# Layer-norm means of the first two tiles in two halves on two engines, and the first load split over two queues

## Chip, cores, metric

The kernel runs on one core of one Trainium2 chip. The metric is device time in microseconds (us). The engines are PE (TensorE), DVE (VectorE), ACT (ScalarE), POOL (GpSimd) and SP (SyncE, which here only starts DMAs).

## The reference

```python
xn = _layernorm(x)                    # x: [1, 2048, 512] bf16, over the last axis
return x + A(xn) + B(xn)              # A: linear attention with softmax features, 32 heads
                                      # B: ((xn @ w_gate) * (xn @ w_up)) @ w_down
```

Everything starts from the layer norm. The kernel works on 16 tiles of 128 tokens by 512. Only the mean has to be subtracted before the first products; the division by the deviation is done later ("deferred").

## The kernel before

A small recording layer notes every operation with its reads and writes; a list scheduler orders each engine, except where `sc.pin` keeps the written order. All that matters here is pinned.

```python
    load_x(0, 2)                      # tiles 0 and 1 in one DMA, 256 KB, SyncE's queue
    load_v(SP, 0)                     # V weights, first half
    load_x(2, 2)                      # tiles 2 and 3
    load_gu(SP, 0, (1,))              # first slice of the up weights
    act(sbf("lnv", 0, 1), eps_f, ["eps"], ["pace"])
    load_v(ACT, 1)                    # V weights, second half, ScalarE's queue
    load_gu(ACT, 0, (0,))             # first slice of the gate weights, ScalarE's queue
    # ... cut ...
    def ln_moments(t):                # VectorE: bn_stats, bn_aggr
        dve(lambda e: e.bn_stats(stats_v[:, t, 0:6], x_tile(t)), [("x", t)], [("st", t)], 512)
        dve(lambda e: e.bn_aggr(mv_v[:, t, :], stats_v[:, t, 0:6]), [("st", t)], [("mv", t)], 1)
    def ln_mean(t):                   # ScalarE: a sum over 512 by the accumulator
        act(xn_tile(t), x_tile(t), [("x", t)], [("mu", t)], scale=1.0 / 512.0, accum=mu[:, t:t + 1])
    # ... cut ...
    warm(7)                           # matmuls on constants, they wait for nothing
    warm(2, 512, [("x", 0)])          # two more once x is there
    sc.pin = True
    ln_moments(0)
    ln_mean(1)
    ln_center(0, 2)                   # x - mean, in two halves
    ln_center(1, 2)
    x_transpose(0, 2, 0, 2)           # four calls: tiles 0 and 1 on PE, by halves
    # ... cut ...
    v_matmul(0, 0)                    # V products of tiles 0 and 1: eight matmuls of 512 columns
    v_matmul(1, 1)
    ln_moments(2)
    ln_mean(3)
    ln_center(2)
    ln_center(3)
    ln_moments(1)
    ln_moments(3)
    # ... PE then: first half of the gate product, transposes of tile 2, next gate half,
    #     transposes of tile 3, and from there a dense stream of matmuls to the end
```

The softmax here doesn't subtract the row's maximum and nothing guards it: scores larger than these inputs give would overflow.

## Time and profile before

| | before |
|---|---|
| time, 3 runs | 221.35 us (221.35 to 221.50) |
| time of the profiled execution | 221.54 us |
| x0 and x1 land / tiles 2 and 3 land | 4.28 / 7.34 us |
| first transpose / first V product / tile 2's transposes | 5.59 / 6.35 / 8.73 us |

Two lines of the page, the span and the chain of work that ended last, by engine:

```profile
span 219.8 us, 3293 instructions
...
PE 96%; DMA 2%; issue 1%; DVE 1%
```

PE sets the time. Next, the timeline of PE alone in the first microseconds: start, duration, engine and line, what it did, and in brackets how long the engine had been idle and what ended that.

```profile
0.82 3.15 PE L640 MATMUL ps<-const-bfloat16-1.0 128*128 128x512 bf16 x7 [0.82 <-PEq L883]
4.32 0.61 PE L640 MATMUL ps<-const-bfloat16-1.0 128*128 128x512 bf16 x2 [0.35 <-DMA arena<-in_A_x_dram]
5.59 0.87 PE L417 MATMUL ps<-arena 128*128 128x128 bf16 x8 [0.66 <-DVE arena L385]
6.35 2.34 PE L222 MATMUL ps<-arena 128*128 128x512 bf16 x12
8.73 0.40 PE L417 MATMUL ps<-arena 128*128 128x128 bf16 x4
8.96 0.60 PE L222 MATMUL ps<-arena 128*128 128x256 bf16 x4
```

L640 are the warm-up matmuls, L417 the transposes. The twelve of L222 are eight V products, 0.216 us apart, and the first gate half, four of 0.109. The single records put the last of these at 8.42, so PE stood still for 0.2 us before 8.73. (Matmul durations overlap: each V product is recorded as 0.38 us long. Distances between starts tell the rate.) What it waited for is on VectorE:

```profile
4.30 0.69 DVE L360 BATCH_NORM_STATS2 arena<-arena 128x6 f32<-128x512 bf16 x1 [4.30 <-DMA arena<-in_A_x_dram]
5.03 0.18 DVE L361 BATCH_NORM_AGGREGATE arena<-arena 128x2 f32<-128x6 f32 x1
5.25 0.87 DVE L385 TENSOR_SCALAR arena<-arena 128x256 bf16<-128x256 bf16 x4
6.30 0.49 DVE L426 COPY arena<-ps 128x256 bf16<-128x256 bf16 x2 [0.18 <-PE ps L417]
7.37 0.69 DVE L360 BATCH_NORM_STATS2 arena<-arena 128x6 f32<-128x512 bf16 x1 [0.58 <-DMA arena<-in_A_x_dram]
8.10 0.18 DVE L361 BATCH_NORM_AGGREGATE arena<-arena 128x2 f32<-128x6 f32 x1
8.32 0.62 DVE L385 TENSOR_SCALAR arena<-arena 128x512 bf16<-128x512 bf16 x2
```

Tile 2 lands at 7.34; its statistics start at 7.37, and aggregate and centering lead to its transposes 1.36 us after that. The transposes start about 0.41 us after VectorE starts centering tile 2 (8.32 and 8.73). So two things meet at 8.73: PE's own work from x0 on, and the load of tile 2.

### The profile page before, as it was taken

To read this page: it belongs to the slowest core of one execution; us is meant where nothing else is said; L and a number is where in the kernel's file an instruction comes from. 1 tells how busy PE (TensorE), PEld (TensorE's weight loads), DVE (VectorE), ACT (ScalarE), POOL (GpSimd) and SP (SyncE) were. 2 spreads that over 40 slices of the span, in tenths; PEclk is the share of its full clock that TensorE was granted. 3 is DMA by queue.
4 is the path that set the end of the run, shared out by engine and by line. 5 is a ranking of instruction groups with operands and counts; after the bars stand their busy time and mean duration, and the time that the engine had idled before them with its cause. 6 is when DMAs were issued, how large, how long until landed. Compare 5 with 4: busy or idle time off the path is not lost.

```text
span 219.8 us, 3293 instructions
## 1 busy us (share of the span) xinstructions
PE 214.4 (98%) x1251; PEld 105.0 (48%) x1275; DVE 141.3 (64%) x245; ACT 86.2 (39%) x162; POOL 53.6 (24%) x119
## 2 busy tenths in 40 slices
PE   6999999999999999999999999999999999999995
PEld 1664444444444444544444444544454444454453
DVE  2766999876546654675486565797766777445341
ACT  4568774787343435333445525531122211000000
POOL 3030553332022202220241422224332222200000
DMA  6999715298200000000002220343764545342221
GB/s 182 295 302 297 198 43 121 59 336 185 49 0 0 0 3 0 0 0 3 0 0 48 49 47 4 71 74 76 163 144 100 118 106 115 87 102 73 61 61 49
DMA packets 47104, 19.90 MB, mean 91 GB/s; under 512 B 37488, under 2 KB 46448, under 8 KB 47088
## 3 DMA queue, kind: packets, MB, share of 16 engines
q1 hardware_dynamic: 46288, 19.16, 36.0%
q10 hardware_dynamic: 800, 0.52, 0.8%
q8 instruction: 10, 0.16, 0.3%
q14 instruction: 6, 0.05, 0.1%
HBM read 8.67 MB, written 2.10 MB: 49 GB/s over the span
## 4 chain that ended last, share of the span: by engine, by line
PE 96%; DMA 2%; issue 1%; DVE 1%
PE ps L222 91%; PE ps L539 2%; PE ps L492 2%; DMA arena<-in_A_x_dram 2%; PE ps L333 1%; PE ps L417 1%; DVE arena L360 0%; DVE arena L385 0%; DVE arena L621 0%; DVE arena L361 0%
## 5 line engine op out<-in xcount | busy, mean ns | idle before, releaser
L222 PE MATMUL ps<-arena 128*128 128x512 bf16 (+3 forms) x938 | 204.8, 371 | 1.3
L222 PEld LDWEIGHTS ps<-arena 128*128 128x128 bf16 x962 | 90.8, 98 | 98.2 <-ACT arena L203 0.2
L203 ACT ACTIVATE arena<-ps 128x512 bf16<-128x512 f32 (+2 forms) x114 | 63.0, 593 | 87.3 <-PE ps L222 74.3
L597 DVE TENSOR_TENSOR arena<-ps,arena 128x512 bf16<-128x512 f32 x56 | 38.5, 687 | 21.8 <-PE ps L222 18.0
L447 DVE TENSOR_REDUCE arena<-arena 128x64 f32<-128x1024 bf16 x32 | 38.5, 1213 | 20.9 <-ACT arena L203 20.9
L457 POOL TENSOR_TENSOR arena<-arena 128x512 bf16<-128x512 bf16 x32 | 33.9, 1060 | 1.3
L455 POOL TENSOR_TENSOR arena<-arena 128x32 f32<-128x32 f32 x32 | 8.6, 268 | 91.2 <-DVE arena L451 50.8
L621 DVE TENSOR_TENSOR arena<-ps,arena 128x512 bf16<-128x512 f32 (+2 forms) x13 | 8.5, 650 | 21.5 <-PE ps L222 21.5
L203 ACT ACTIVATE arena<-arena 128x512 bf16<-128x512 bf16 (+3 forms) x29 | 14.4, 508 | 5.8 <-DMA arena<-in_A_x_dram 2.8
L360 DVE BATCH_NORM_STATS2 arena<-arena 128x6 f32<-128x512 bf16 x16 | 10.4, 674 | 5.0 <-DMA arena<-in_A_x_dram 4.9
L203 ACT ACTIVATE arena<-ps,arena 128x512 bf16<-128x512 f32 x16 | 10.1, 685 | 5.7 <-PE ps L222 5.7
L560 DVE TENSOR_TENSOR arena<-ps,arena 128x512 bf16<-128x512 f32 x16 | 11.1, 691 | 0.6
L480 DVE TENSOR_TENSOR arena<-ps,arena 128x512 bf16<-128x512 f32 x16 | 10.3, 643 | 0.0
L451 DVE RECIPROCAL arena<-arena 128x64 f32<-128x64 f32 x16 | 8.4, 533 | 0.0
L492 PEld LDWEIGHTS ps<-arena 128*128 128x128 bf16 x128 | 6.2, 97 | 3.8
L539 PEld LDWEIGHTS ps<-arena 128*128 128x128 bf16 x128 | 6.2, 97 | 3.8
L397 POOL TENSOR_SCALAR arena<-arena 128x1 f32<-128x1 f32 x12 | 3.0, 269 | 17.7 <-ACT arena L203 17.7
L539 PE MATMUL ps<-arena 128*128 128x68 bf16 x128 | 6.7, 194 | 0.0
L492 PE MATMUL ps<-arena 128*128 128x68 bf16 x128 | 6.7, 194 | 0.0
L559 DVE RECIPROCAL arena<-arena 128x32 f32<-128x32 f32 x16 | 5.6, 353 | 0.5
L453 DVE RECIPROCAL arena<-arena 128x32 f32<-128x32 f32 x16 | 5.4, 344 | 0.2
L474 POOL CAST arena<-arena 128x32 bf16<-128x32 f32 x16 | 5.2, 322 | 0.0
(30 smaller groups left out, 34.0 us busy)
## 6 DMA issues: line engine op xcount, KB each, us to landing
out_dram<-arena SPq DMA_DIRECT2D x15, 128.0 KB, 1.7
arena<-in_B_w_down_dram SPq DMA_DIRECT2D x1, 1792.0 KB, 8.0
arena<-in_A_x_dram SPq DMA_DIRECT2D x3, 512.0 KB, 3.7
arena<-arena SPq DMA_TRANSPOSE x44, 2.8
arena<-in_B_w_gate_dram SPq DMA_DIRECT2D x1, 640.0 KB, 8.9
arena<-in_B_w_up_dram SPq DMA_DIRECT2D x1, 640.0 KB, 10.0
arena<-in_A_x_dram SPq DMA_DIRECT2D x2, 256.0 KB, 4.6
arena<-in_B_w_gate_dram SPq DMA_DIRECT2D x1, 512.0 KB, 5.4
```

The lines of the kernel that those rows point to most:

```text
L203: return sc.step(ACT, lambda e: e.activation(out=out_ap, in_=in_ap, func=func, scale=scale, **kw), reads, writes, 130.0 + 0.833 * n)
L222: ins = e.matmul(out_ap, lhsT=l, rhs=r, start=start and i == 0, stop=stop and i == npair - 1, **kw)
L360: dve(lambda e: e.bn_stats(stats_v[:, t, 0:6], x_tile(t)), [("x", t)], [("st", t)], 512)
L447: dve(lambda e: e.tensor_reduce(out=sm, in_=e_v, axis=AX.X, op=ALU.add), [(name, s, 0), (name, s, 1)], [("sums", sr)], 1024)
L455: pool(lambda e: e.tensor_tensor(out=rat, in0=sm[:, :, 0], in1=rs[:, :, 1], op=ALU.mult), [("sums", sr), ("rs", s)], [("rat", s)], 32)
L457: pool(lambda e: e.tensor_tensor(out=e_v[:, :, 1, :], in0=e_v[:, :, 1, :], in1=rat[:, :, None].to_broadcast([128, H, 16]), op=ALU.mult), [ ...
L480: dve(lambda e: e.tensor_tensor(out=vs_tile(t)[:, :, 0:16], in0=bank(b).rearrange("p (h f) -> p h f", h=H), in1=rp.unsqueeze(2).to_broadca ...
L492: ins = e.matmul(bank(c // 4, (c % 4) * CW, CW), lhsT=ek[:, c * 128:(c + 1) * 128], rhs=vs[:, c * CW:(c + 1) * CW], start=(t == 0 and c % ...
L539: ins = e.matmul(bank(b0 + c // 4, (c % 4) * CW, CW), lhsT=ph[:, c, :], rhs=kvz_v[:, c, :], start=True, stop=True)
L560: dve(lambda e: e.tensor_tensor(out=o_tile(t).rearrange("p (b h f) -> p b h f", b=2, f=16), in0=nd[:, :, :, 0:16], in1=w_v[:, r].unsqueeze ...
L597: dve(lambda e: e.tensor_tensor(out=hT_v[:, ft, sg * 512:(sg + 1) * 512], in0=bank(bu), in1=g, op=ALU.mult), [("ps", bu), ("g", s)], [("hT ...
L621: dve(lambda e, ps=ps, stg=stg, cs=cs: e.tensor_tensor(out=stg, in0=ps, in1=x_tile(t)[:, cs], op=ALU.add), [("ps", bk), ("x", t)], [("ostg ...
```

## The change

The intent: center tile 0 sooner, by loading it alone and by summing its two halves on two engines at once, and push the statistics, needed only later, out of the way.

```diff
-    load_x(0, 2)
+    load_x(0, 1)
+    load_x(1, 1, ACT)
...
+    def ln_mean_split(t):
+        act(xn_tile(t)[:, 256:], x_tile(t)[:, 256:], [("x", t)], [("mu", t)], scale=1.0 / 512.0,
+            accum=mu[:, t:t + 1])
+        dve(lambda e: e.tensor_scalar(out=xn_tile(t)[:, :256], in0=x_tile(t)[:, :256], scalar1=1.0 / 512.0,
+                                      scalar2=0.0, op0=ALU.mult, op1=ALU.add, accum_out=mua[:, t:t + 1]),
+            [("x", t)], [("mua", t)], 256)
+    def ln_center_split(t):
+        for h in range(2):
+            hs = slice(h * 256, (h + 1) * 256)
+            dve(lambda e, hs=hs: e.tensor_scalar(out=xn_tile(t)[:, hs], in0=x_tile(t)[:, hs], scalar1=mua[:, t:t + 1],
+                                                 scalar2=mu[:, t:t + 1], op0=ALU.subtract, op1=ALU.subtract),
+                [("x", t), ("mua", t), ("mu", t)], [("xn", t, h)], 256, 0.27)
...
-    warm(2, 512, [("x", 0)])
+    warm(1, 512, [("x", 0)])
     sc.pin = True
-    ln_moments(0)
-    ln_mean(1)
-    ln_center(0, 2)
-    ln_center(1, 2)
+    ln_mean_split(0)
+    ln_center_split(0)
+    ln_mean_split(1)
+    ln_center_split(1)
...
     v_matmul(1, 1)
+    ln_moments(0)
     ln_moments(2)
```

The change also takes one warm-up matmul away, and it puts a load ahead of V's and the gate weights on ScalarE's queue.

More of the change, by code (lines that the diff above doesn't have):

```diff
@@ L162, in _build @@
     alloc("mu", 2 * ND)
+    alloc("mua", 2 * ND)
     alloc("nrstd", 2 * ND)
@@ L375, in ln_stats @@
         sc.prio = 1
+    mua = sbf("mua", 0, ND)
+    def ln_mean_split(t):
[10 more added lines that the diff above has]
+                [("x", t), ("mua", t), ("mu", t)], [("xn", t, h)], 256, 0.27)
     def ln_mean(t):
```

## The prediction

> **What bounds the kernel now.** The tensor engine: the page's busy shares give PE 98% of a 219.8 us span; the chain that ended last is 96% PE. From 5.59 us on, the timeline of the matmuls shows nearly no hole. So the change can win only before about 9 us; nothing later gets shorter.
>
> **The start before (timeline, chain).** The 256 KB load of tiles 0 and 1 is issued at 0.79 us and lands at 4.28. VectorE: statistics 4.30 (0.69 us), aggregate 5.03 (0.18), four centerings 5.25 to 6.12. PE: transposes 5.59, V products 6.35 (eight of 0.216), first gate half 8.09 to 8.53, then a hole of 0.2 us, and tile 2's transposes at 8.73. That hole is a second bound: tiles 2 and 3 land at 7.34, and statistics, aggregate and centering of tile 2 take 1.36 us from there.
>
> **The change, costed.**
> - x0 alone is 128 KB. The packet records show x0 and x1 in 2 KB packets of about 84 ns, first at 1.82, typically done by 2.9, slowest 3.9. Half of it should land at about 3.6 (3.3 to 4.0). x1, from ScalarE's queue, at about 4.0. [...] the two queues' loads are served in order of issue (ScalarE's first packet starts at 2.96, as x's load ends). The order changes: tiles 2 and 3 now come before the first gate weights, 256 KB earlier; at the 330 GB/s of these microseconds about 0.7 us, so at 6.6, while gate weights slip from 6.63 to 7.3.
> - Half a mean: ScalarE 0.33 + 0.18 = 0.51 us (512 elements took 0.72), VectorE about 0.45 at the same time, in place of 0.95 for statistics and aggregate. Tile 0's centering starts at about 4.2.
> - Tile 1 gains less: its VectorE half stands behind tile 0's centerings; it is centered by about 5.5.
> - Moved, not removed: tile 0's statistics and aggregate (0.95 us) now stand ahead of tile 2's on VectorE, from about 6.2 to 7.1. So tile 2's statistics start at about 7.1 instead of 7.37, though x is there at 6.6.
> - One warm-up matmul of 0.22 us goes from a hole: free.
>
> **On the critical path.** Transposes of tile 0 come about 1 us earlier, V products and gate half 0.6; then PE waits for tile 2, whose transposes come only 0.2 to 0.4 us earlier. The whole PE stream behind shifts by that. Most of what is won in front is lost in that wait.
>
> **Predicted:** 221.05 us (0.3 us less), range 220.4 to 221.6. Faster by over 2%: 1%; within 2%: 98.5%; slower: 0.5%.
>
> **What would show each step.** x0 landing near 3.6; first centering 4.2; first transpose 4.5; V products 5.7; x2 landing 6.6; tile 2's statistics 7.1, right behind the moved ones; a hole of 0.4 to 0.6 us before tile 2's transposes, at 8.3 to 8.5; everything after shifted alike.
>
> **What would make it wrong.** ScalarE's issue may wait behind its table load, or its packets interleave with x0's; the accumulating VectorE half may be slow (over 0.5 us); late V or gate weights may hold PE; the PE clock: [...] Here matmuls went from 0.427 us apart to 0.22 between 3.3 and 4.5 us; less warm-up could delay that. Other instruction orders later, from the list scheduler, could move some tenths either way.

Two passages, on the queues and on the PE clock, are cut where marked, because no trace of this case shows what they said. The sum comes to 221.05 us, 0.3 less than 221.35.

## The result

221.63 us (median of 6, 221.28 to 222.14) against 221.41 (6 runs, 221.35 to 221.50). The ratio is 1.0011, interval 0.9997 to 1.0024. A ratio is the mean time of one kernel's runs over that of the other's runs of the same rounds, so not quite the ratio of the medians quoted. That is the same time within noise, 0.2 us up instead of 0.3 down, and just above the stated range (221.6). What stands out is the spread: 0.86 us where the kernel before had 0.15.

The profiled execution happened to be the fastest, 221.28 us. Its page:

```profile
span 219.5 us, 3324 instructions
...
PE 95%; DVE 2%; DMA 1%; issue 0%; ACT 0%; DVEq 0%
```

PE alone:

```profile
0.82 3.57 PE L658 MATMUL ps<-const-bfloat16-1.0 128*128 128x512 bf16 x8 [0.82 <-PEq L902]
4.50 0.62 PE L435 MATMUL ps<-arena 128*128 128x128 bf16 x4
5.47 0.54 PE L435 MATMUL ps<-arena 128*128 128x128 bf16 x4 [0.36 <-DVE arena L391]
5.85 2.46 PE L223 MATMUL ps<-arena 128*128 128x512 bf16 x12
8.41 0.40 PE L435 MATMUL ps<-arena 128*128 128x128 bf16 x4
8.64 0.60 PE L223 MATMUL ps<-arena 128*128 128x256 bf16 x4
```

And VectorE (L384 is the half mean, L391 the centering with two scalars, L362 the statistics: first tile 0's, then tile 2's):

```profile
3.48 0.42 DVE L384 TENSOR_SCALAR_CACHE_REDUCE arena<-arena 128x256 bf16<-128x256 bf16 x1 [3.48 <-DMA arena<-in_A_x_dram]
3.82 0.08 DVE L384 DVE_READ_ACCUMULATOR arena<-arena 128x1 f32 x1
4.10 0.60 DVE L391 TENSOR_SCALAR arena<-arena 128x256 bf16<-128x256 bf16 x2 [0.19 <-ACT arena L204]
4.61 0.41 DVE L384 TENSOR_SCALAR_CACHE_REDUCE arena<-arena 128x256 bf16<-128x256 bf16 x1
4.95 0.08 DVE L384 DVE_READ_ACCUMULATOR arena<-arena 128x1 f32 x1
5.07 0.60 DVE L391 TENSOR_SCALAR arena<-arena 128x256 bf16<-128x256 bf16 x2
...
6.26 0.69 DVE L362 BATCH_NORM_STATS2 arena<-arena 128x6 f32<-128x512 bf16 x1
6.98 0.18 DVE L363 BATCH_NORM_AGGREGATE arena<-arena 128x2 f32<-128x6 f32 x1
7.08 0.66 DVE L362 BATCH_NORM_STATS2 arena<-arena 128x6 f32<-128x512 bf16 x1
7.77 0.18 DVE L363 BATCH_NORM_AGGREGATE arena<-arena 128x2 f32<-128x6 f32 x1
7.99 0.62 DVE L403 TENSOR_SCALAR arena<-arena 128x512 bf16<-128x512 bf16 x2
```

In this execution nearly every step came as forecast: first centering 4.10, V products 5.85, x2 landing 6.69, its statistics 7.08 right behind the moved ones, its transposes 8.41. Against the profiled execution of before that is 0.32 us at the transposes and 0.26 us in time (221.28 against 221.54). So the question is not whether that chain exists but what the other executions do.

**One rule for all runs.** Sixteen profiles were taken in the end. In each, the time is the start of tile 2's transposes plus 212.81 to 212.94 us. Behind that point all the kernels run alike; only what comes before it counts.

| kernel | warm-ups | gate weights by | x2 lands | gate weights land | tile 2's transposes | time of that run | difference |
|---|---|---|---|---|---|---|---|
| before | 9 | ScalarE | 7.34 | 6.63 | 8.73 | 221.54 | 212.81 |
| after | 8 | ScalarE | 6.69 | 7.66 | 8.41 | 221.28 | 212.87 |
| r1_after | 8 | ScalarE | 7.80 | 9.22 | 10.29 | 223.18 | 212.89 |
| r2_warm | 9 | ScalarE | 6.67 | 8.04 | 8.53 | 221.38 | 212.85 |
| r3_gate_behind | 8 | SyncE | 6.90 | 7.79 | 9.84 | 222.69 | 212.85 |
| r4_load_only | 9 | ScalarE | 6.83 | 7.83 | 8.32 | 221.26 | 212.94 |
| r5_before_warm1 | 8 | ScalarE | 7.45 | 6.70 | 8.82 | 221.64 | 212.82 |
| r6_stats_behind | 9 | ScalarE | 7.95 | 9.38 | 9.87 | 222.73 | 212.86 |
| r7_mean_only | 9 | ScalarE | 7.22 | 6.51 | 9.11 | 221.93 | 212.82 |
| r8_warm4 | 11 | ScalarE | 7.49 | 8.92 | 9.41 | 222.28 | 212.87 |
| r9_gate_fill | 9 + 1 | SyncE | 6.40 | 7.34 | 8.61 | 221.47 | 212.86 |
| r10_fill | 9 + 1 | ScalarE | 7.35 | 8.50 | 8.99 | 221.84 | 212.85 |
| r11_gate_fill_behind | 9 + 1 | SyncE | 6.42 | 7.27 | 7.98 | 220.83 | 212.85 |
| r12_split_one_queue | 9 + 1 | ScalarE | 7.42 | 5.98 | 9.06 | 221.94 | 212.88 |
| r13_gate_nine | 9 | SyncE | 6.43 | 7.34 | 8.67 | 221.55 | 212.88 |
| r14_load_gate | 9 | SyncE | 6.28 | 7.10 | 8.33 | 221.17 | 212.84 |

(Landings are the last of the 16 completions of a load in the trace's landing records; "+ 1" is a warm-up matmul between the transposes of tiles 0 and 1.)

### The profile page after: what moved, and what is told of

The parts are those of the page before. It is cut to its first block, busy times and chain, and to the rows that moved or that the text cites. A ratio compares the mean times of both kernels' runs of the same rounds, so it can differ in the third digit from the quotient of the medians.

```text
span 219.5 us, 3324 instructions
## 1 busy us (share of the span) xinstructions
PE 215.8 (98%) x1274; PEld 105.0 (48%) x1274; DVE 142.2 (65%) x249; ACT 86.4 (39%) x164; POOL 53.6 (24%) x119
## 3 DMA queue, kind: packets, MB, share of 16 engines
HBM read 8.67 MB, written 2.10 MB: 49 GB/s over the span
## 4 chain that ended last, share of the span: by engine, by line
PE 95%; DVE 2%; DMA 1%; issue 0%; ACT 0%; DVEq 0%
PE ps L223 90%; PE ps L557 2%; PE ps L510 2%; DMA arena<-in_A_x_dram 1%; PE ps L335 1%; DVE arena L362 1%; PE ps L435 0%; DVE arena L391 0%; DVE arena L444 0%; ACT arena L204 0%; DVE arena L384 0%; DVE arena L363 0%; DVE arena L403 0%; DVE arena L639 0%; DVEq L875 0%
## 5 line engine op out<-in xcount | busy, mean ns | idle before, releaser
L223 PE MATMUL ps<-arena 128*128 128x512 bf16 (+3 forms) x962 | 207.2, 371 | 0.0
L223 PEld LDWEIGHTS ps<-arena 128*128 128x128 bf16 x962 | 90.8, 98 | 98.3 <-DMA arena<-in_B_w_gate_dram 0.5
L204 ACT ACTIVATE arena<-arena 128x512 bf16<-128x512 bf16 (+4 forms) x30 | 14.6, 497 | 5.3 <-POOL arena L415 2.6
L362 DVE BATCH_NORM_STATS2 arena<-arena 128x6 f32<-128x512 bf16 x16 | 10.4, 671 | 0.3 <-DMA arena<-in_A_x_dram 0.3
L568 POOL TENSOR_SCALAR arena<-arena 128x32 f32<-128x32 f32 x4 | 1.2, 293 | 16.3 <-DVE arena L465 16.3
```

The lines of the kernel that those rows point to most:

```text
L204: return sc.step(ACT, lambda e: e.activation(out=out_ap, in_=in_ap, func=func, scale=scale, **kw), reads, writes, 130.0 + 0.833 * n)
L223: ins = e.matmul(out_ap, lhsT=l, rhs=r, start=start and i == 0, stop=stop and i == npair - 1, **kw)
```

## The experiments

Each kernel ran five timed rounds beside the kernel before on the same chip; all gave correct results.

| kernel | median (range), runs | before, same chip | ratio (95% interval) |
|---|---|---|---|
| r1_after | 222.12 (221.23 to 223.18), 6 | 221.35 | 1.0033 (1.0008 to 1.0058) |
| r2_warm | 221.57 (221.38 to 221.64), 5 | 221.35 | 1.0007 (0.9995 to 1.0019) |
| r3_gate_behind | 221.98 (221.17 to 223.07), 6 | 221.35 | 1.0030 (1.0002 to 1.0058) |
| r4_load_only | 221.61 (221.26 to 221.70), 5 | 221.35 | 1.0011 (0.9998 to 1.0024) |
| r5_before_warm1 | 221.61 (221.49 to 222.85), 6 | 221.45 | 1.0023 (1.0003 to 1.0043) |
| r6_stats_behind | 221.79 (221.09 to 222.73), 6 | 221.45 | 1.0017 (1.0000 to 1.0033) |
| r7_mean_only | 221.91 (221.58 to 223.00), 6 | 221.45 | 1.0025 (1.0009 to 1.0040) |
| r8_warm4 | 221.88 (221.48 to 222.65), 6 | 221.45 | 1.0018 (1.0004 to 1.0033) |
| r9_gate_fill | 221.34 (221.22 to 221.47), 5 | 221.50 | 0.9995 (0.9982 to 1.0007) |
| r10_fill | 221.90 (221.79 to 222.06), 5 | 221.50 | 1.0020 (1.0007 to 1.0032) |
| r11_gate_fill_behind | 221.09 (220.83 to 221.35), 5 | 221.50 | 0.9986 (0.9973 to 1.0000) |
| r12_split_one_queue | 221.94 (221.90 to 222.16), 5 | 221.50 | 1.0023 (1.0010 to 1.0035) |
| r13_gate_nine | 221.43 (221.32 to 221.55), 5 | 221.42 | 1.0001 (0.9988 to 1.0013) |
| r14_load_gate | 220.87 (220.56 to 221.17), 5 | 221.42 | 0.9974 (0.9961 to 0.9988) |

### First call: what makes the runs differ?

**r1_after**: the changed kernel, unaltered.

> The changed kernel again, for its spread (its six runs gave 221.28 to 222.14 us, those of the kernel before 221.35 to 221.50). Theory LOADS: the loads of tiles 2 and 3 (SyncE, issued at 1.71 us) and of the first gate weights (ScalarE, issued at 1.74 us) are in a tie, and which is served first differs from run to run; where the gate weights go first, x2 lands some 0.7 us later and with it all that follows. It expects the same spread again, 221.2 to 222.2, and, if the profile falls on a slow run, x2 landing at 7.2 or later in place of 6.69. Theory CLOCK: the work now starts before the matmul clock is up in some runs; then a slow run shows V products 0.427 us apart in place of 0.216, and x2 at 6.7. Theory NOISE: the spread was chance, and all runs lie at 221.2 to 221.5.

The spread is real and wider: 221.23, 221.31, 221.70, 222.54, 222.81, 223.18. The profile caught the slowest. PE in it:

```profile
0.82 3.57 PE L658 MATMUL ps<-const-bfloat16-1.0 128*128 128x512 bf16 x8 [0.82 <-PEq L902]
4.71 0.65 PE L435 MATMUL ps<-arena 128*128 128x128 bf16 x4 [0.31 <-DVE arena L391]
5.68 0.65 PE L435 MATMUL ps<-arena 128*128 128x128 bf16 x4 [0.32 <-DVE arena L391]
6.13 4.33 PE L223 MATMUL ps<-arena 128*128 128x512 bf16 x12
10.29 0.39 PE L435 MATMUL ps<-arena 128*128 128x128 bf16 x4
```

The same twelve matmuls of L223 take 4.33 us instead of 2.46. The single records show all eight V products 0.427 us apart, and the gate half 0.213: half rate until about 10.2 us. In the fast execution the rate had doubled between 4.84 and 5.47. NOISE falls. The eight V products lose eight times 0.211 us, 1.7 in all, but not all of it reaches tile 2, because in the same profile x2 (7.80) and the gate weights (9.22) are over a microsecond late too. In r6 and r8 below, where the V products run at full rate, tile 2's transposes start 0.49 us after the gate weights land. By that the landing alone would have put them at about 9.7 here (an estimate). So of the 1.9 us between 223.18 and 221.28 about 1.3 goes with the landing, and the half rate adds the last 0.6.

**r2_warm**

```diff
-    warm(1, 512, [("x", 0)])
+    warm(2, 512, [("x", 0)])
```

> The changed kernel with the ninth warm-up matmul given back. CLOCK expects the spread to vanish, all runs at 221.2 to 221.4 us. LOADS expects the same spread as r1_after, 221.2 to 222.2.

The spread went (0.26 us), as CLOCK says. The level, 221.57, is above its forecast of 221.2 to 221.4 and above before. In the profile, PE waits 0.24 us for the gate weights, which land at 8.04.

**r3_gate_behind**

```diff
-    load_gu(SP, 0, (1,))
+    load_gu(SP, 0)
...
-    load_gu(ACT, 0, (0,))
```

> The changed kernel with the load of the first gate weights taken from ScalarE's queue and put on SyncE's, behind the load of tiles 2 and 3, so that there is no tie. LOADS expects x2 to land at 6.3 to 6.8 us in every run, the spread to shrink to 0.3 us or less and the median to lie at 221.0 to 221.4. CLOCK and NOISE expect no change against r1_after.

LOADS, in this form, fell: x2 landed at 6.90 close to what it expected, but the runs are 221.17, 221.26, 221.28, 222.69, 222.92, 223.07. The profile (222.69) again has V products 0.427 us apart, up to 9.1 us. Here the landings are not to blame: VectorE starts centering tile 2 at 8.30, so its transposes could have come at about 8.7 (an estimate, by the 0.41 us above) instead of 9.84. The late clock cost about 1.1 us. But note the gap: nothing lies between 221.28 and 222.69. The in-between runs of the changed kernel (221.55 to 221.85) are missing here.

**r4_load_only**: the kernel before with `load_x(0, 1)` and `load_x(1, 1, ACT)` alone.

> The kernel before with the split load alone (x0 on SyncE, x1 on ScalarE; statistics, mean and warm-up as before). LOADS expects the spread here too: about 220.7 us where x2 lands at 6.7, because tile 2's statistics then start as x2 lands, with nothing moved ahead of them, and up to 221.6 where the gate weights go first. CLOCK expects no spread, as the nine warm-up matmuls and the later first transpose (about 4.8 us) are there.

No slow runs (CLOCK), but no 220.7 either: 221.61. In its profile, of its fastest run (221.26), PE waits 0.45 us for the gate weights, which land at 7.83. VectorE starts centering tile 2 at 7.81, so without that wait its transposes would have come at about 8.22 (an estimate) instead of 8.32. So a second bound showed that neither theory had: the gate weights. In this run it is worth 0.1 us; the other four runs (221.56 to 221.70) have no profile.

### Second call: clock or start, statistics, and the parts alone

**r5_before_warm1**: the kernel before with `warm(1, ...)` for `warm(2, ...)`.

> The kernel before with one warm-up matmul fewer (one after x0 lands, not two), nothing else. So far the two runs of the changed start with eight warm-up matmuls that a profile caught at 223.18 and 222.69 us had the clock up only at about 10.2 and 9.4 us, and nine warm-up matmuls gave 221.38 to 221.64 in all of five runs. CLOCK (the missing ninth matmul decides): slow runs appear here too, some at 222 to 223 us. Rival START (the missing matmul is harmless by itself; what counts is that the work of the changed start comes earlier, with a hole between the transposes of tiles 0 and 1): all runs stay at 221.2 to 221.6.

Two of six runs are at 222.80 and 222.85; START falls. The kernel before has 1 such run in 47 (222.69; the other 46 lie between 221.22 and 221.72). The profile fell on a fast run (221.64), so that these two had the clock late is inferred from r1 and r3, not seen.

**r6_stats_behind**

```diff
-    warm(1, 512, [("x", 0)])
+    warm(2, 512, [("x", 0)])
...
-    ln_moments(0)
     ln_moments(2)
     ln_mean(3)
     ln_center(2)
     ln_center(3)
+    ln_moments(0)
     ln_moments(1)
```

> The changed kernel with nine warm-up matmuls, and tile 0's statistics moved on, from ahead of tile 2's to behind the centering of tiles 2 and 3. If the moved statistics bound r2_warm (tile 2's transposes at 8.53 us, its statistics started 0.5 us after x2 landed), tile 2's statistics now start as x2 lands (6.7 us), its transposes come at about 8.1 to 8.2, and the time falls by 0.2 to 0.4 us against r2_warm (221.57), to about 221.25. If the landing of the first gate weights (8.0 us in r2_warm) binds, the transposes still wait for the gate half, at about 8.5, and the time stays at 221.5.

Its second branch came, and worse: gate weights at 9.38, a wait of 1.39 us on PE for them, 222.73 in that run, with the V products at full rate. One run reached 221.09.

**r7_mean_only**: the changed kernel with `load_x(0, 2)` and nine warm-ups.

> The kernel before with the mean in halves and the moved statistics alone: one load of tiles 0 and 1 as before, nine warm-up matmuls. x0 lands at 4.28 us, the first centering comes at about 4.9 in place of 5.25, but tile 2 lands at 7.34 as before and tile 0's statistics now end at about 7.9, so tile 2's transposes should come at about 9.1 in place of 8.73: 221.7 us, 0.35 slower than before. If the moved statistics did no harm it would be 221.0 to 221.35. The clock: nine warm-up matmuls, so no slow runs.

Tile 2's transposes at 9.11, as computed; 221.91. So without the earlier load of tile 2 the moved statistics show their whole cost. "No slow runs" missed: one of six is at 223.00, and no profile shows why.

**r8_warm4**: the changed kernel with `warm(4, ...)`.

> The changed kernel with eleven warm-up matmuls in place of eight. CLOCK: no slow runs. As the front has 0.5 us of room before tile 2's transposes, the later first transpose (5.2 to 5.5 us in place of 4.5) should cost nothing: 221.3 to 221.6, as r2_warm. If warm-up matmuls themselves cost time there (r2_warm's median of 221.57 is above the fast runs of r1_after, 221.23 to 221.31), it is 221.8 or more.

221.88 has the number of the second branch, but not its cause, and the one run at 222.65 that "no slow runs" excluded has no profile. V products begin at 6.37 and could have ended in time; the gate weights land at 8.92. The landings explain the profiled run (222.28), not the warm-up matmuls.

**What the landings show.** These are the 16 completions of one load, in order, for tiles 2 and 3:

```
before          6.62 6.66 6.73 6.83 6.84 6.86 6.87 6.89 6.94 7.00 7.03 7.07 7.11 7.22 7.24 7.34
after           5.67 5.79 5.89 6.13 6.16 6.18 6.23 6.30 6.31 6.39 6.44 6.45 6.46 6.57 6.66 6.69
r1_after        5.66 5.69 5.74 5.81 5.85 5.91 5.92 5.96 5.97 6.04 6.14 6.21 6.23 7.32 7.64 7.80
r6_stats_behind 5.47 5.49 5.52 5.63 5.69 5.70 5.83 5.86 5.96 5.97 5.98 6.01 6.19 6.96 7.01 7.95
```

A load counts as landed with the last one (before: 7.34, and tile 2's statistics start at 7.37). Before, the 16 keep within 0.72 us; in r1 they are spread over 2.14 (5.66 to 7.80). With x on both queues most of them come a microsecond sooner, but in some runs one to three stay behind by about 1 to 2 us, and the gate weights behind them likewise. A spread of 1.5 us or more was seen in four profiles (r1, r6, r8, r10), all with x1 and the gate weights both on ScalarE's queue. In the five with the gate weights on SyncE's (r3, r9, r11, r13, r14) it is 0.6 to 1.3 us, though x is on both queues there too.

### Third call: cure both

**r9_gate_fill**: r3's loads, nine warm-up matmuls, and one more (`warm(1)`) after the transposes of tile 0.

> By now all ten profiled runs obey one rule: time = start of tile 2's transposes on PE + 212.85 us (within 0.1). So each run's time is set by what comes before that point. Two causes of lateness were seen: CLOCK (V products 0.427 us apart up to 9.4 or 10.2 us: r1_after, r3_gate_behind) and LANDING (the first gate weights land at 8.9 to 9.4 us in place of 7.7, x2 at 7.5 to 8.0 in place of 6.7: r1_after, r6_stats_behind, r8_warm4; never where x0 and x1 come as one load). This kernel takes away both at once: nine warm-up matmuls and one more in the hole between the transposes of tiles 0 and 1, and the first gate weights on SyncE's queue behind tile 2 (in r3_gate_behind they landed at 7.8, and its runs were either 221.17 to 221.28 or above 222.6, nothing between). If both causes are right and these are all: no run above 221.6, median 221.2 to 221.35, tile 2's transposes at 8.3 to 8.6. If a run above 222 remains, one of them is not cured or a third is there.

A hit: 221.22 to 221.47, transposes at 8.61. With both causes taken away neither the slow runs nor the ones between are left in these five. The clock is not early in this profile, only early enough: the second V product starts 0.43 us after the first, the third 0.22 us after the second.

**r10_fill**: the same, gate weights on ScalarE's queue as in the change.

> The changed kernel with nine warm-up matmuls and the one in the hole; gate weights on ScalarE's queue as in the change. LANDING alone is left: most runs 221.3 to 221.9, some to 222.7; the profile shows V products 0.216 us apart from 6.5 us or earlier, and time = start of tile 2's transposes + 212.85. If CLOCK were the only cause, all runs would lie at 221.2 to 221.6.

221.90, in a narrower range (221.79 to 222.06) than expected. The V products are at full rate from 6.38 on. PE in it:

```profile
6.00 2.06 PE L223 MATMUL ps<-arena 128*128 128x512 bf16 x8
8.55 0.61 PE L223 MATMUL ps<-arena 128*128 128x256 bf16 x4 [0.49 <-DMA arena<-in_B_w_gate_dram]
```

The gate half waits for its weights, to 8.55. Beside r9 on the same chip, the queue of this one load, and with it its place among the loads, is worth 0.56 us.

**r11_gate_fill_behind**: r9 with tile 0's statistics moved behind, as in r6.

> r9_gate_fill with tile 0's statistics moved behind the centering of tiles 2 and 3. If nothing but x2's landing is left, tile 2's transposes come 1.36 us after it, or when the first gate half is done (gate weights at 7.8, so 8.2): about 8.2 to 8.3 us, 221.05 to 221.15, some 0.15 to 0.3 below r9_gate_fill and 0.2 to 0.4 below the kernel before. If the moved statistics cost nothing there, it equals r9_gate_fill.

221.09, 0.25 below r9; transposes at 7.98, directly behind the gate half. So the moved statistics cost about 0.25 us where the loads are in time; with five runs each, which overlap (220.83 to 221.35 against 221.22 to 221.47), the size is rough.

**r12_split_one_queue**: r10 with both x loads on SyncE's queue.

> r10_fill with x0 and x1 loaded one after the other by SyncE, so that ScalarE's queue carries only weights, as in the kernel before. If what makes the late landings is x on both queues (V's and gate weights then being served side by side with x2), landings are as before: x2 at 7.2 to 7.5, first gate weights at 6.5 to 6.8, the 16 queues of one load within 0.8 us of each other, all runs within 0.3 us of each other, and time about 221.4 to 221.6, because tile 2's statistics start at about 7.3. If splitting the load is enough by itself to spread the 16 queues, gate weights or x2 lands late by a microsecond here too.

The landings are a hit: x2 at 7.42 with its 16 within 0.45 us, gate weights at 5.98, runs within 0.26 us. The time is a miss (221.94), for two reasons that end together at tile 2's transposes (9.06). The first half of the V weights, now third on SyncE's queue, lands at 6.71 and holds the V products to 6.85. And x1 lands only at 5.09, which puts tile 0's moved statistics at 6.92 and tile 2's at 7.74, 0.3 us after x2. Splitting by itself did not spread the 16 here.

### Fourth call: which part cures, which part earns

**r13_gate_nine**: r9 without the matmul in the hole.

> r3_gate_behind (three of six runs above 222.6 us) with the ninth warm-up matmul given back, and nothing in the hole between the transposes. If the ninth matmul alone cures the late clock, all runs lie at 221.2 to 221.5, as in r9_gate_fill. If the matmul in the hole was needed, some run lies above 222 again, or the profile shows V products 0.427 us apart beyond 7 us.

221.32 to 221.55: the ninth warm-up matmul is enough in these five runs, though its profile shows the rate doubling only at about 6.0 us.

**r14_load_gate**: the kernel before with r3's loads; statistics and means as before.

> The kernel before with x0 and x1 split over two queues and the first gate weights on SyncE behind tile 2, but with the old statistics in the old place (no mean in halves, nothing moved). If the mean in halves earns something at tile 2, this is slower than r11_gate_fill_behind (221.09). If it earns nothing, because tile 2 waits for its own load and statistics: x2 at 6.4 to 6.8, its statistics at once, its transposes 1.36 us after x2 at 7.8 to 8.2, time 220.7 to 221.1, as fast as r11 or faster.

220.87, ratio 0.9974 (0.9961 to 0.9988): below the kernel before clear of noise, though by 0.26% only, and the fastest kernel here. PE and VectorE in its profile (a run of 221.17, its slowest):

```profile
4.92 1.04 PE L417 MATMUL ps<-arena 128*128 128x128 bf16 x8
5.79 2.70 PE L222 MATMUL ps<-arena 128*128 128x512 bf16 x12
8.33 0.39 PE L417 MATMUL ps<-arena 128*128 128x128 bf16 x4
```

```profile
3.63 0.69 DVE L360 BATCH_NORM_STATS2 arena<-arena 128x6 f32<-128x512 bf16 x1 [3.63 <-DMA arena<-in_A_x_dram]
4.36 0.18 DVE L361 BATCH_NORM_AGGREGATE arena<-arena 128x2 f32<-128x6 f32 x1
4.58 0.87 DVE L385 TENSOR_SCALAR arena<-arena 128x256 bf16<-128x256 bf16 x4
...
6.30 0.69 DVE L360 BATCH_NORM_STATS2 arena<-arena 128x6 f32<-128x512 bf16 x1
```

There is no wait left between the V products and tile 2. The first three V products start 0.40 us apart, the next 0.22, so in this run the rate doubled only at about 6.6 us; at full rate it would have come some 0.37 us sooner (an estimate), near the median. Beside r13, which differs only in the means and the statistics and ran on the same chip, it is 0.56 us faster. So the main part of the change costs time: 0.25 of it was measured as the moved statistics (r11 against r9), and the profiles show where some more goes. VectorE ends the centering of both tiles 1.84 us after x0 lands in the kernel before (4.28 to 6.12) and in r14 (3.61 to 5.45), but 2.22 in the changed kernel (3.45 to 5.67) and 2.23 in r13. Tile 0's centering starts sooner (0.65 us after landing instead of 0.97). But VectorE now does the two tiles one after the other, with a half mean (0.42 us and 0.08) between, and a centering with two scalars takes 0.34 us instead of 0.28. And in the pinned order PE transposes both tiles before its first V product (5.85 in the changed kernel).

## Why the prediction was wrong

- **Right: the bound, and that most of the gain would be lost at tile 2.** x0 at 3.45 (said 3.6), V products 5.85 (5.7), x2 6.69 (6.6), its statistics 7.08 (7.1), transposes 8.41 (8.3 to 8.5), a wider hole before them.
- **Off: the base of the sum.** The 0.3 us was the distance to a trace whose own run took 221.54, taken from a median of 221.35. By the rule above, 221.35 means transposes at about 8.50 (221.35 less 212.85), not 8.73. So the gain against typical runs was about 0.1 us: the changed kernel's fastest runs are 221.23 to 221.35.
- **Wrong, the failing step for the slow third of the runs: "One warm-up matmul of 0.22 us goes from a hole: free."** It was not free. With eight warm-up matmuls (changed kernel, r1, r3, r5) 8 of 24 runs are at 222.5 us or more; with nine or more, 3 of 58 runs of the altered kernels (one of them, in r6, by the gate weights as its profile shows) and 1 of 47 of the kernel before. Two of the 8 are in profiles, both with V products at half rate up to 9.1 us or later. The prediction named the clock as a risk, without a size; the V products lose up to 1.7 us by it, and the time about 0.6 us in r1 and 1.1 in r3 (estimates, above).
- **Wrong, and most likely what set the result's median: gate weights "slip from 6.63 to 7.3", with no wait for them in the sum.** Late weights, too, were named as a risk without a size. They were 7.66 to 9.38 on ScalarE's queue behind x1, and held PE up by 0.24 us or more in five profiles with the clock up in time (r2, r4, r6, r8, r10). Of that wait, 0.02, 0.10, 0.54, 0.54 and 0.26 us reached tile 2's transposes (estimates, by the 0.41 us after VectorE's centering). On SyncE's queue (r3, r9, r11, r13, r14) they landed at 7.1 to 7.8. Landing times were computed as bytes over a mean rate; that leaves out how the last of the 16 parts of a load fares. None of the result's six runs is at 222.5 us or more; four lie between 221.55 and 222.14. With the ninth warm-up matmul given back and nothing else, r2 still has 221.57; with the gate weights moved, r3 has no run between 221.28 and 222.69. So the result's median is put down to the gate weights and not to the clock; its runs between 221.55 and 222.14 have no profile, so this is inferred.
- **And with both cured the change as made wins nothing.** r9 and r13 only equal the kernel before (ratios 0.9995 and 1.0001); the base of the sum (above) and tile 1 (below) are what is left to account for the forecast 0.3 us.
- **Mis-sized: "Tile 1 gains less."** Measured from the landing of x0, tile 1 loses 0.38 us (2.22 against 1.84). The part that the change is named for earns nothing at the point that sets the time.

On the clock, the traces show when the rate changed, not what decides it. The same program doubled its rate at about 5 us in one run and at about 10.2 in another (V products 0.216 us apart in the first, 0.427 in the second). Thirteen of the traces hold clock records. Full clock is granted from 4.03 to 6.44 us on in eleven runs, all but one with nine or more warm-up matmuls; the one is the fast changed run, from 4.95. It is granted from 9.26 in r3 and from 10.18 in r1. How much work on PE brings the full clock was not shown: no run varied that alone. So the ninth matmul's worth rests on the counts of runs above, and why it helps stays open.

On the queues, the loads of both were seen to interleave: in the fast changed run, packets of x2 (4.58 to 6.19 us) and of the gate weights (from 5.19 on) run side by side. And moving one load from one queue to the other, and so in the order of loads, changed the time by 0.56 us (r9, r10).

**Open.** Why one to three of the 16 fall behind when x1 and the gate weights share ScalarE's queue. What decides when the full clock comes, and why the kernel before, which also has a hole in its warm-up (PE idle 0.35 us before 4.32), is late in only 1 of 47 runs. With nine or more warm-up matmuls none of the 35 runs of r2 and r9 to r14 is above 222.2, but r7 had one run at 223.00 and r8 one at 222.65 unseen by a profile.

## What to carry to other kernels

Where a start is a race of several chains, find the one point behind which all runs are alike, and judge each change by when that point comes; here sixteen profiles gave one constant. Look at the spread of runs and at more than one profile before you price a gain of tenths: a lucky or unlucky trace misled here by as much as the effect. A warm-up matmul in a hole was insurance here, not waste (8 of 24 runs at 222.5 us or more with eight, 3 of 58 with nine or more), and the last of a load's 16 completions, not its bytes, decided when the consumer started (in r1 the last part of x2 came at 7.80, its statistics at 7.83).
